# Linear attention with a relu-squared MLP on one core: six chunk pairs instead of four, most of them beside attention, streamed weights, and key sums in turning DVE passes

## The chip, the cores and the metric

The kernel runs on one core of one Trainium2 chip. The metric is the device time of a whole execution in microseconds, the median of several runs. TensorE is called PE, VectorE DVE, ScalarE ACT, GpSimd POOL, and SyncE, which issues most DMAs, SP.

## The reference

```python
def phi(x):                                      # q, k: [8, 8, 576, 64]
    proj = np.einsum('bhsd,df->bhsf', x, w_phi)  # w_phi: [64, 128]
    proj = proj - np.max(np.abs(proj), axis=-1, keepdims=True)
    return np.concatenate([np.exp(proj), np.exp(-proj)], axis=-1)
q_p, k_p = (phi(q), phi(k))
kv = np.einsum('bhsf,bhsd->bhfd', k_p, v)
z = np.sum(k_p, axis=2)
num = np.einsum('bhsf,bhfd->bhsd', q_p, kv)
den = np.einsum('bhsf,bhf->bhs', q_p, z)[..., None] + 1e-06
x = (num / den).transpose(0, 2, 1, 3).reshape(4608, 512)
r = np.maximum(x @ w_in, 0.0)                    # w_in: [512, 2048]
return (r * r) @ w_out                           # w_out: [2048, 512]
```

Attention has no softmax: the key features give a small matrix kv and a vector z, the key sum, for each of the 64 heads. Its output x goes through an MLP of 4608 tokens.

## The kernel before, in words

**Attention** works on 32 pairs of heads. The first six go through `early()`; the other 26 are each spread over *visits* of PE (`visit()`): Q and the key projection of the next pair (L884, L611), the last tokens (L892, L617), then kv of this pair (L669, L674), and the numerators of the pair before (L904). These use half-height or half-width tiles of PE, into the PSUM banks pn, pv, pp and pz. `keys()` takes the key projection out of PSUM, subtracts the largest magnitude and exponentiates (tiles e, and et for the last 64 tokens), and starts the key sums: DVE folds e's token blocks into tile es (L650, L655), and adds et (L660), for each head. `late()` turns es in 32x32 blocks (L966), reduces it to 16 numbers a partition (L967), and sends these through DRAM (zd) and back to be summed into zc (L974). POOL reduces over partitions twice a head: the largest magnitude of a query (L982) and the denominators (L1003). `tokens()` writes x as two float16 halves, high and low, into a *ring* of chunks.

**The MLP** cuts the tokens into 18 chunks of 256 and the hidden columns into 8 steps f of 256. In a plain step (`moe()`) gemm1 makes 24 matmuls with a 128x128 piece of w_in and 256 tokens, float16 in three products of high and low (L1051); ACT takes the relu out of bank ph (L1060); `squares()` makes the square's high part gh on ACT and the low part gl on DVE (a subtraction by the helper at L331); gemm2 adds 12 matmuls of 512 columns to the bank po of the chunk (L1088). A *pair step* (`pair()`) does gemm1 for two chunks at once by seven products of 2x2 blocks instead of eight: 42 matmuls (L1233) instead of 48. It wants sums of blocks of w_in (`add_w()`) and of x (`add_x()`) beforehand, and block sums afterwards: ACT copies one product, DVE makes four adds (L1248), and ACT takes two relus (L1265) before the squares.

Before, 10 chunks are plain and run beside attention; the other 8 form four pairs after it, the first three steps of the first pair being plain. The ring holds 7 chunks, so three of them wait in DRAM (`spill()`, `reload()`). All of w_in stays in two tiles.

**The order of the work** is fixed before the kernel runs: every piece is an operation with the engine, its dependencies, its buffers and a rank, and `Plan` takes for each engine the ready operation of least rank. The ranks come from the table RANKS, two characters an operation. Each engine has its instructions in that one static order, and SP's DMA issues are one such list. Where PE would have stood still early in the program, fillers are put, matmuls on zeros.

## Time and profile before

| what | value |
| --- | --- |
| three runs | 1019.7, 1020.3 and 1021.87 us, median 1020.3 |
| the profiled execution | span 1018.5 us, 1.8 below the median of the runs |
| PE, matmuls | 999.8 us busy, 98% |
| DVE | 763.2 us, 75% |
| ACT | 680.5 us, 67% |
| POOL | 361.2 us, 35% |
| DMA | 77.34 MB, 76 GB/s on the mean |

The span is one execution from its first to its last instruction; busy times come from that execution. An engine's share of busy time is a mean over stages: 0 to 123 us before the first visit, the visits until 705 us, and from there on pairs of chunks alone. Matmuls overlap on PE, so what one costs is read from the distance of two starts.

### The profile page before, as it was taken

How to read it: one execution, taken by the hardware profiler on the slowest of the kernel's cores; microseconds unless marked ns; L12 is line 12 of the kernel's file. 1: busy time of each engine (PE TensorE's matmuls, PEld its weight loads, DVE VectorE, ACT ScalarE, POOL GpSimd, SP SyncE). 2: the span in 40 equal slices, each digit the busy share in tenths (PEclk: the TensorE clock that was granted, in tenths of full speed). 3: DMA queues.
4: the chain of work that ended last, by engine and by line, in shares of the span. 5: the costliest groups of instructions: out<-in, count | busy, mean ns of one | idle time of the engine just before them, and what ended most of it. 6: DMA issues, size and time to landing. Idle time of an engine off the chain costs nothing.

```text
span 1018.5 us, 19261 instructions
## 1 busy us (share of the span) xinstructions
PE 999.8 (98%) x7632; PEld 694.6 (68%) x7713; DVE 763.2 (75%) x1221; ACT 680.5 (67%) x1206; POOL 361.2 (35%) x138
## 2 busy tenths in 40 slices
PE   8999999999999999999999999999999999999998
PEld 4657776776666667666767666666776767677675
DVE  5899878798878989777879888798888447343432
ACT  6989886777777787686777867776555445435444
POOL 2433356364456555475375646563000000000000
PEclk9999999999999999999999999999999999999999
DMA  9754323132322233233324212110002001000001
GB/s 355 282 186 135 122 81 94 39 110 73 85 60 81 75 93 93 60 82 81 107 80 111 83 48 69 41 41 22 13 2 83 1 1 49 14 1 21 22 1 42
DMA packets 94914, 77.34 MB, mean 76 GB/s; under 512 B 58088, under 2 KB 72424, under 8 KB 92776
## 3 DMA queue, kind: packets, MB, share of 16 engines
q1 hardware_dynamic: 94536, 75.59, 24.6%
q8 instruction: 60, 0.98, 0.4%
q10 hardware_dynamic: 288, 0.52, 0.1%
q14 instruction: 30, 0.25, 0.1%
HBM read 61.16 MB, written 14.78 MB: 75 GB/s over the span
## 4 chain that ended last, share of the span: by engine, by line
PE 90%; DVE 3%; DMA 3%; ACT 2%; issue 1%; SPq 0%; DVEq 0%; ACTq 0%
PE po L1088 27%; PE ph L1051 21%; PE pp L1233 7%; PE pz L669 4%; PE pv L1088 4%; PE pn L1088 4%; PE ph L1233 3%; PE pn L904 3%; PE pn L884 2%; PE pp L611 2%; PE pv L904 2%; PE pz L1233 2%; PE pz L674 1%; PE pv L669 1%; PE pz L892 1%
## 5 line engine op out<-in xcount | busy, mean ns | idle before, releaser
L1051 PE MATMUL ph<-ring,win 128*128 128x256 f16 x2064 | 240.4, 273 | 0.8 <-ACT r L1060 0.8
L1051 PEld LDWEIGHTS <-win 128*128 128x128 f16 x2064 | 195.3, 98 | 47.0 <-issue 24.8
L982 POOL PARTITION_ALL_REDUCE mx<-pt x52 | 121.6, 2339 | 122.7 <-ACT pt L335 84.3
L1088 PE MATMUL po<-wh,gh 128*128 128x512 f32 x448 | 143.8, 442 | 0.0
L1003 POOL PARTITION_ALL_REDUCE rb<-rb x26 | 96.5, 3712 | 112.0 <-DVE rb L1000 95.6
L1265 ACT ACTIVATE qe<-qe,cw 128x512 f32<-128x512 f32 x58 | 41.4, 715 | 112.5 <-DVE qe L1248 112.5
L1088 PE MATMUL po<-wl,gl 128*128 128x512 bf16 x448 | 115.1, 379 | 0.0
L331 DVE TENSOR_TENSOR gl<-r,gh 128x512 bf16<-128x512 f32 x86 | 87.5, 1018 | 31.7 <-ACT r L1070 30.7
L1003 POOL PARTITION_ALL_REDUCE ds<-ds x26 | 98.7, 3797 | 25.2 <-DVE ds L1000 24.5
L1088 PE MATMUL po<-wl,gh 128*128 128x512 bf16 x375 | 101.5, 379 | 4.9 <-issue 1.6
L1088 PEld LDWEIGHTS <-gl 128*128 128x128 bf16 x576 | 56.4, 98 | 68.0
L1088 PEld LDWEIGHTS po<-wh,gh 128*128 128x128 f32 x448 | 84.6, 189 | 25.9
L1248 DVE TENSOR_TENSOR qe<-pp,qe 128x512 f32<-128x512 f32 (+1 forms) x87 | 52.3, 602 | 61.3 <-PE pp L1233 59.5
L1060 ACT ACTIVATE r<-ph,cw 128x512 f32<-128x512 f32 x86 | 58.7, 683 | 51.0 <-PE ph L1051 49.3
L331 DVE TENSOR_TENSOR gl<-qe,gh 128x512 bf16<-128x512 f32 x58 | 40.1, 691 | 65.7 <-ACT qe L1070 65.6
L1088 PEld LDWEIGHTS <-gh 128*128 128x128 bf16 x576 | 52.3, 98 | 50.7 <-issue 8.9
L633 ACT ACTIVATE e<-e 128x512 f32<-128x512 f32 x64 | 40.0, 625 | 32.3 <-DVE e L630 32.3
L1233 PEld LDWEIGHTS <-win 128*128 128x128 f16 x522 | 48.8, 98 | 14.2 <-issue 7.8
L1068 ACT ACTIVATE gh<-r 128x512 fp32r<-128x512 f32 x86 | 54.1, 629 | 5.7 <-PE pv L1088 2.0
L1070 ACT ACTIVATE r<-r 128x512 f32<-128x512 f32 x86 | 54.3, 631 | 2.7
L650 DVE TENSOR_TENSOR es<-e 128x512 f32<-128x512 f32 x52 | 46.3, 890 | 4.5 <-ACT e L635 4.3
L669 PE MATMUL pz<-e,v 128*64 128x256 f32 x416 | 49.3, 379 | 0.0
(286 smaller groups left out, 1970.4 us busy)
## 6 DMA issues: line engine op xcount, KB each, us to landing
...
out_dram<-o SPq DMA_DIRECT2D x34, 256.0 KB, 2.1
...
spill<-ring SPq DMA_DIRECT2D x6, 256.0 KB, 2.9
```

Source lines behind the costliest of these rows:

```text
L331: eng.tensor_tensor(out=out_, in0=a, in1=b_, op=ALU.subtract)
L669: PE.matmul(out=to[64 * h:64 * h + 64, 0:256], lhsT=v_[p][:, t, h, :], rhs=e_[2 * p + h][:, t].rearrange("p s f -> p (s f)"), start=t == 0 ...
L904: PE.matmul(out=to[64 * h:64 * h + 64, :], lhsT=kz_[n][:, 128 * s_ + 64 * h:128 * s_ + 64 * h + 64], rhs=qe_[2 * n + h].rearrange("p (s x) ...
L982: o = P.add("POOL", par_us(S), lambda n=n, h=h: G.partition_all_reduce(mx_[n], pt_[p][:, h, :], channels=128, reduce_op=bass_isa.ReduceOp. ...
L1003: o = P.add("POOL", 3.6, lambda y=y: G.partition_all_reduce(y(), y(), channels=128, reduce_op=bass_isa.ReduceOp.add), [o], [home], R(RQ + ...
L1051: PE.matmul(out=ph[:, j, :], lhsT=win[w][:, t, 128 * ff:128 * ff + 128], rhs=at_ring(c, x, t), start=k == 0, stop=k == 3 * KT - 1)
L1060: o = P.add("ACT", act_us(512, 1), lambda: A.activation(out=r_[n], in_=ph_[bank], func=AF.Relu, scale=cw[:, f, 0:1]), [g1], [("ph", bank), ...
L1068: sq = P.add("ACT", act_us(512), lambda: A.activation(out=gh_[n], in_=r(), func=AF.Square), after, use + [("gh", n)], Q)
L1070: o = P.add("ACT", act_us(512), lambda: A.activation(out=r(), in_=r(), func=AF.Square), [sq], use, Q, other=[("DVE", 0.70, lambda: V.tenso ...
L1088: PE.matmul(out=bank(i), lhsT=x[:, j, 128 * i:128 * i + 128], rhs=w[:, j, :], start=turn + j + s == 0, stop=(turn, j, s) == (NFP - 1, 1, 2))
L1233: PE.matmul(out=to, lhsT=fl(x, *al)(k), rhs=fr(y, *ar)(k), start=n == 0, stop=n == 5)
L1248: V.tensor_tensor(out=to, in0=a, in1=b, op=ALU.add)
```

## The change

Key sums: from pair 6 on, three DVE passes take the place of eight instructions. Each is a reduce with `apply_transpose`, which turns 32x32 blocks as it reads them and sums 32 elements: one for each head's e (128x1024 elements), one for et (128x256). The 72 numbers a partition go to zd and come back by two DMAs into the end of kz, and zc is reduced from there. DVE's subtraction for et goes too: ACT exponentiates it from PSUM with a bias, for which it negates the largest magnitude (kmn).

Chunks: 6 are plain, 12 form six pairs, so 48 steps are pair steps and none of these pairs has plain steps. Five pairs (MID) run beside attention, as far as it lasts. Their steps put the seven products into the banks ph, pn, pv and again ph, pn and pv being those of the visits; a copy on ACT takes the first product out, and DVE has one add for each of the other three banks, two for pv. The gh and gl of the pair's second chunk go to DRAM (`put_away()`) and come back (`take_back()`) for its gemm2 after the eight steps of the first. The last pair uses pz, pp and ph, and gemm2 of both chunks directly.

Weights: w_in lies in one tile for each f. It is stored to DRAM (wd), the sums of its blocks are made ahead, half an f at a time, and stored as well (`ahead()`), and `weights()` loads both parts for each pair step, 512 KB each, into two alternating sets of tiles. The ring holds 8 chunks and nothing is spilled. The table RANKS is new and covers all operations; STAY, what a change of tile shape costs a rank, falls from 6 to 0.

Over the whole program there are now 3168 matmuls of gemm1 (1152 plain, 2016 in pair steps) instead of 3282 (2064 and 1218), as many of gemm2 as before, 29 fillers instead of 13, and 713 DMA issues on SP instead of 419. Up to the first visit there are 192 matmuls of gemm1 instead of 168, and the 16 more fillers lie there.

```diff
-RING = 7 * T
+RING = 8 * T
-PAIRED = 10
-PLAIN = 3
-SPILLED = (10, 11, 12)
-PAIRS = ((13, 14), (15, 16), (17, 10), (11, 12))
-TAIL = LEAD + (STEP - 1.0) * PAIRED * NFP
+PAIRED = 6
+PAIRS = [(c, c + 1) for c in range(PAIRED, NCH, 2)]
+MID = 5
...
+        if p >= EARLY:
+            def fold(src, col, k, after, use, rank):
+                sums[p].append(P.add("DVE", dve_us(256 * k), lambda: V.tensor_reduce(
+                    out=col(), in_=src().rearrange("p k (b x) -> p k b x", x=32), op=ALU.add, axis=AX.X, apply_transpose=True),
+                    [after], [use, ("z4", p)], rank))
+
+            for h in range(2):
+                n = 2 * p + h
+                fold(lambda n=n: e_[n].rearrange("p t s f -> p (t s) f"),
+                     lambda h=h: z4_[p][:, :, 0:16].rearrange("p b (u h x) -> p h u x b", u=2, h=2)[:, h],
+                     4, exps[p][h], ("e", n), R(1.0))
+            fold(lambda: et_[p], lambda: z4_[p][:, :, 16:18].rearrange("p b s -> p s b"), 1, exp_t[p], ("et", p), R(1.0))
...
-        o = P.add("DVE", dve_us(512), lambda: V.transpose(es_[p][:, 512:1024], es_[p][:, 0:512]), sums[p], [("es", p)], R(RZ))
-        o = P.add("DVE", dve_us(512), lambda: V.tensor_reduce(
-            out=z4_[p].rearrange("p (b c) -> p c b", c=4), in_=es_[p][:, 512:1024].rearrange("p (c b x) -> p c b x", c=4, x=32), op=ALU.add, axis=AX.X),
-            [o], [("es", p), ("z4", p)], R(RZ))
-
-        o = P.add("SP", 0.4, lambda: SP.dma_start(zd_[p], z4_[p]), [o], [("z4", p), ("zd", p)], R(RZ), land=1.9, xfer=0.1)
-        o = P.add("SP", 0.55, lambda: SP.dma_start(za_[p], zd_[p].rearrange("(a i) (b c) -> (i b) a c", a=4, b=4)),
-                  [o], [("zd", p), ("za", p)], R(RZ), land=2.2, xfer=0.3)
+        w = P.add("SP", 0.4, lambda: SP.dma_start(zd_[p], z4_[p]), sums[p], [("z4", p), ("zd", p)], R(RZ), land=1.9, xfer=0.1)
+        back = []
+        back.append(P.add("SP", 0.5, lambda: SP.dma_start(
+            kz_[p][:, 256:320].rearrange("p (a x) -> p a x", a=4),
+            zd_[p].rearrange("(a i) b x -> (i b) a x", a=4)[:, :, 0:16]), [w], [("zd", p), ("kz", p)], R(RZ), land=2.1, xfer=0.1))
+        back.append(P.add("SP", 0.5, lambda: SP.dma_start(
+            kz_[p][:, 320:328].rearrange("p (a s) -> p a s", a=4),
+            zd_[p].rearrange("(a i) b x -> (i b) a x", a=4)[:, :, 16:18]), [w], [("zd", p), ("kz", p)], R(RZ), land=2.1, xfer=0.2))
         zc = P.add("DVE", 0.23, lambda: V.tensor_reduce(
-            out=zc_[p], in_=za_[p].rearrange("p a c -> p c a"), op=ALU.add, axis=AX.X),
-            [o], [("za", p), ("zc", p)], R(RZ))
+            out=zc_[p], in_=kz_[p][:, 256:328].rearrange("p (y h x s) -> p h s y x", h=2, x=2, s=2), op=ALU.add, axis=AX.XY),
...
+    def weights(f, rank):
+        b = in_pair["step"] = in_pair.get("step", 1) ^ 1
+        o = P.add("SP", 0.45, lambda: SP.dma_start(wo_at(b), wd_[f][0]), [w_stored[f]] + read_o[b], [WO[b]], rank, land=2.4, xfer=1.4)
+        if f in s_stored:
+            s = P.add("SP", 0.45, lambda: SP.dma_start(ws_at(b).rearrange("p k n x c -> p k (n x c)"), wd_[f][1]), s_stored[f] + read_s[b], [WS[b]], rank, land=2.4, xfer=1.4)
+            read_o[b], read_s[b] = [], []
+            return b, [o, s]
...
+    def step(cs, k, turn, f, n, m):
+        g = in_pair["n"] = in_pair.get("n", -1) + 1
+        Q = m - 1000.0
+        rt, r = RT[g % 2], lambda: r_at(g % 2)
+        b, w_ready = weights(f, m - 5.0)
+        product = factors(cs, b)
+        grid = lambda x: x.rearrange("p (j t) -> p j t", j=2)
+        after = w_ready + [parts_x[cs, i] for i in range(2)] + in_pair.get("pe", [])
...
+        i0 = in_pair["ph"]
+        if k < MID:
+            in_pair["ph"] += 2
+            keys = [("ph", i0)], [("pn", ("b", g))], [("pv", ("b", g))], [("ph", i0 + 1)]
+            banks = [lambda: ph_[i0], lambda: grid(pn_["b", g]), lambda: grid(pv_["b", g]), lambda: ph_[i0 + 1]]
+        else:
+            in_pair["ph"] += 1
+            px = ("pp", ("w", g))
+            keys = [("pz", ("w", g))], [px], [px], [("ph", i0)]
+            banks = [lambda: grid(pz_["w", g]), lambda: grid(pp_["w", g][:, 0, :]), lambda: grid(pp_["w", g][:, 1, :]), lambda: ph_[i0]]
+        two = lambda i, x, y: lambda: (product(banks[i]()[:, 0, :], *x), product(banks[i]()[:, 1, :], *y))
+        pa = P.add("PE", 0.66, lambda: product(banks[0]()[:, 0, :], "a11", "b11"), after, keys[0] + reads, m)
+        first, other = copy(T, lambda: r()[:, 1, :], lambda: banks[0]()[:, 0, :])
+        ca = P.add(*first, [pa] + old, keys[0] + [rt], Q - URGENT, other=[other])
+        pb = P.add("PE", 1.31, two(1, ("a12", "b21"), ("s2", "t2")), [pa], keys[1] + reads, m + 0.01)
+        cb_ = P.add("DVE", dve_us(512), lambda: plus(r()[:, 0:4:3, :], banks[1](), wide(r()[:, 1, :])), [ca, pb], keys[1] + [rt], Q - URGENT)
+        pc = P.add("PE", 1.31, two(2, ("s3", "t3"), ("s1", "t1")), [pb], keys[2] + reads, m + 0.02)
+        cc_ = P.add("DVE", dve_us(512), lambda: plus(r()[:, 1:3, :], banks[2](), wide(r()[:, 3, :])), [cb_, pc], keys[2] + [rt], Q - URGENT)
+        c22 = P.add("DVE", dve_us(T), lambda: plus(r()[:, 3, :], banks[2]()[:, 0, :], r()[:, 2, :]), [cc_], keys[2] + [rt], Q - URGENT)
+        pd = P.add("PE", 1.31, two(3, ("a22", "t4"), ("s4", "b22")), [pc], keys[3] + reads, m + 0.03)
+        cd = P.add("DVE", dve_us(512), lambda: plus(r()[:, 1:3, :], banks[3](), r()[:, 1:3, :]), [pd, cc_], keys[3] + [rt], Q - URGENT)
+        in_pair["pe"] = [pd]
...
+            done.append(squares(n + i, lambda i=i: r()[:, 2 * i:2 * i + 2, :], [x], [rt], Q + 0.1 * i))
         in_pair["r", g] = done
+        return done
+
+    gone, read_back = {}, {}
+
+    def put_away(n, k, f, g, rank):
+        def work():
+            SP.dma_start(gd_[k % 2][f][0], gh_[n].bitcast(F32))
+            SP.dma_start(gd_[k % 2][f][1], gl_[n])
+
+        gone[k, f] = P.add("SP", 0.9, work, [g] + read_back.get((k - 2, f), []), [("gh", n), ("gl", n)], rank, land=2.0, xfer=1.1)
+
+    def take_back(n, k, f, rank):
+        def work():
+            SP.dma_start(gh_[n].bitcast(F32), gd_[k % 2][f][0])
+            SP.dma_start(gl_[n], gd_[k % 2][f][1])
+
+        o = P.add("SP", 0.9, work, [gone[k, f]], [("gh", n), ("gl", n)], rank, land=2.2, xfer=1.1)
+        read_back[k, f] = [o]
+        return o
...
+        later = [("po", po0 + 2 + i) for i in range(2)] if mid else [("pn", ("o", k)), ("pv", ("o", k))]
+        po0 += 4 if mid else 2
+        turn_us *= 1.4 if mid else 1.9
+        for j in range(NFP):
+            done = step(cs, k, j, j, n, m)
+            second(n, cs[0], v, j, j, done[0], m + 2.5, po)
+            if mid:
+                put_away(n + 1, k, j, done[1], m)
             else:
...
+                second(n + 1, cs[1], v + 1, j, j, done[1], m + 3.5, later)
+            n += 2
+            m += turn_us
+        used = list(in_pair["pe"])
+        for j in range(NFP if mid else 0):
+            o = take_back(n, k, j, m)
+            second(n, cs[1], v + 1, j, j, o, m + 1.5, later)
+            n += 1
+            m += tick * 0.5
+        v += 2
...
-    "L=6CLUTFEO2uPvAD.-.-Ht3`E*LhX{c?L|81TPLM/%B1.CGQn<cD>of`k:Rv35E9p?e$W-WMWIrtOQ1OhEaM9p48lUaroXtSqqwO"
...
+    "1x3&75;HDe0h0h<07<:>6[@)BS8iE8>>899k<REj>a?B3?4h4n?2@05T<%.T6J6o>{Is?[@2?-6;9S:x>.>Z9O;W=0;*B]BY?*:>"
...
```

**DVE, key sums of a late pair, before.** Names: es folded exponentials, et the last tokens, qe and ds the denominators of other pairs, gl a square of the MLP, z_12 the key sum.

```order
L650 TENSOR_TENSOR es_4663<-e_4601 128x512
L655 TENSOR_TENSOR es_4663<-es_4663 128x256
L660 TENSOR_TENSOR es_4663<-es_4663,et_4625 64x256
L1000 SCALAR_TENSOR_TENSOR rb_4751<-qe_4634,zc_4689,pp_4696 128x576
L966 STREAM_TRANSPOSE es_4663<-es_4663 128x512
L331 TENSOR_TENSOR gl_4762<-r_4748,gh_4753 128x512
L1000 SCALAR_TENSOR_TENSOR ds_4795<-qe_4725,zc_4689,pp_4760 128x576
L967 TENSOR_REDUCE z_12_4815<-es_4663 128x4x4
```

These are the folds of the second head, the transpose and the reduce; the same two folds and the add of the first head stand a few rows earlier.

**DVE, key sums of a late pair, after**, at the same stage of the program; e_4545 and e_4551 are the two heads of one pair.

```order
L628 TENSOR_REDUCE km_4547<-pp_4506 128x4
L631 TENSOR_TENSOR e_4551<-pp_4506,km_4547 128x4x128
L660 TENSOR_REDUCE z_10_4563<-e_4545 128x2x4x4
L650 TENSOR_REDUCE kmt_4576<-pz_4523 128x1
L959 STREAM_TRANSPOSE kvs_4578<-pz_4523 128x256
L660 TENSOR_REDUCE z_10_4563<-e_4551 128x2x4x4
L841 TENSOR_TENSOR rb_4339<-n_4612,rb_4339 128x576
L329 TENSOR_TENSOR qe_4619<-pt_4540,mx_4569 128x576
L660 TENSOR_REDUCE z_10_4563<-et_4582 128x2x4
```

The three rows of L660 with z_10 are all that is left of the sums, and each stands as soon as its e or et is exponentiated.

**DVE, a pair step, before**, after the end of attention (qe_8746 holds the block sums, pp and ph are the banks).

```order
L1248 TENSOR_TENSOR qe_8746<-pp_9815,qe_8746 128x512 x2
L1248 TENSOR_TENSOR qe_8746<-ph_9842,qe_8746 128x512
L1248 TENSOR_TENSOR qe_8746<-pp_9815,qe_8746 128x256
L331 TENSOR_TENSOR gl_9891<-qe_8746,gh_9887 128x512
L1176 TENSOR_TENSOR es_8168<-ring_0_78,ring_1_79 128x2x256
L1176 TENSOR_TENSOR es_8168<-ring_1712 128x2x256
L331 TENSOR_TENSOR gl_9918<-qe_8746,gh_9893 128x512
```

**DVE, a pair step, after**, beside attention: w_1_4650 and w_1_5294 hold the block sums, in the second use of tiles w0 and w1; pn, pv and ph are the banks, and qe_6674, ds_6760 and pt belong to attention.

```order
L329 TENSOR_TENSOR qe_6674<-pt_6375,mx_6599 128x576
L329 TENSOR_TENSOR gl_6699<-w_1_5294,gh_6672 128x512
L1249 TENSOR_TENSOR w_1_4650<-pn_6685,w_1_4650 128x2x256
L1249 TENSOR_TENSOR w_1_4650<-pv_6704,w_1_4650 128x512
L1249 TENSOR_TENSOR w_1_4650<-pv_6704,w_1_4650 128x256
L1249 TENSOR_TENSOR w_1_4650<-ph_6719,w_1_4650 128x512
L329 TENSOR_TENSOR gl_6755<-w_1_5294,gh_6702 128x512
L1006 SCALAR_TENSOR_TENSOR ds_6760<-qe_6674,zc_6657,pp_6737 128x576
L329 TENSOR_TENSOR gl_6789<-w_1_4650,gh_6764 128x512
```

The four adds now stand between a query's subtraction, a denominator's product (L1006) and the squares' subtractions of the step before and of the same step (gl).

**PE, a visit, before**: kv of one pair (pz), the numerators of the pair before (pn, pv), and the next gemm1.

```order
L669 MATMUL pz_5611<-e_5440,v_4402 64x256
L674 MATMUL pz_5611<-et_5446,v_4402 64x256 x2
L904 MATMUL pn_5638<-qe_5448,kz_5481 64x320
L904 MATMUL pn_5638<-qe_5508,kz_5481 64x320
...
L904 MATMUL pv_5639<-qe_5448,kz_5481 64x256
L904 MATMUL pv_5639<-qe_5508,kz_5481 64x256
...
L1051 LDWEIGHTS win_76
L1051 MATMUL ph_5670<-ring_1712,win_76 128x256
```

**PE, a visit, after**: behind kv come the products of a pair step,

```order
L674 MATMUL pz_5809<-e_5487,v_4566 64x256
L674 MATMUL pz_5809<-e_5507,v_4566 64x256
L679 MATMUL pz_5809<-et_5599,v_4566 64x256 x2
L1243 LDWEIGHTS w_1_4901
L1243 MATMUL ph_5839<-ring_1761,w_1_4901 128x256
```

and the numerators follow some hundred rows later, behind a gemm2.

```order
L1075 MATMUL po_5346<-wl_1240,gl_5836 128x512
L1075 MATMUL po_5343<-wh_1232,gh_5828 128x512 x2
L1075 MATMUL po_5346<-wh_1232,gh_5828 128x512 x2
L910 MATMUL pn_5972<-qe_5472,kz_5699 64x320
L910 MATMUL pn_5972<-qe_5530,kz_5699 64x320
...
L910 MATMUL pv_5973<-qe_5472,kz_5699 64x256
L910 MATMUL pv_5973<-qe_5530,kz_5699 64x256
```

In 10 of the 26 visits the numerators are split off so, before in 2.

## Rows read from the trace of the kernel before

**Rows 1.** The page: the span, and each engine's busy time.

```profile
span 1018.5 us, 19261 instructions
PE 999.8 (98%) x7632; PEld 694.6 (68%) x7713; DVE 763.2 (75%) x1221; ACT 680.5 (67%) x1206; POOL 361.2 (35%) x138
```

**Rows 2.** The page: shares of the chain that ended last, by engine.

```profile
PE 90%; DVE 3%; DMA 3%; ACT 2%; issue 1%; SPq 0%; DVEq 0%; ACTq 0%
```

**Rows 3.** Windows: us, then busy us of PE, PEld, DVE, ACT, POOL; clock, DMA share, GB/s.

```profile
0.00:122.60 122.60, 114.78 (x1140) 76.31 (x1148) 101.10 (x173) 105.70 (x184) 40.33 (x32) 0.99 0.63 224
122.60:705.00 582.40, 578.78 (x4498) 402.21 (x4541) 492.19 (x778) 426.59 (x787) 319.50 (x106) 1.00 0.28 75
705.00:782.00 77.00, 74.99 (x495) 53.14 (x500) 66.74 (x108) 39.69 (x61) 1.40 (x1) 1.00 0.10 32
782.00:1018.50 236.50, 231.30 (x1506) 162.97 (x1527) 103.16 (x164) 108.54 (x176) 0.00 (x0) 1.00 0.05 16
350.00:400.00 50.00, 49.52 (x402) 33.73 (x402) 45.93 (x70) 37.06 (x72) 28.36 (x10) 1.00 0.34 89
```

**Rows 4.** PE's timeline in the tail: start, duration, line, operation, count.

```profile
827.40 0.61 PE L1088 MATMUL pn<-wl,gh 128*128 128x512 bf16 x2
...
830.08 0.83 PE L1233 MATMUL pz<-ring,win 128*128 128x256 f16 x6
...
831.40 0.49 PE L1233 MATMUL pp<-k,qe 128*128 128x256 f16 x3
...
832.38 0.49 PE L1233 MATMUL pp<-q,qe 128*128 128x256 f16 x3
```

**Rows 5.** PE's timeline at visit 517: a gemm1, then Q.

```profile
517.79 2.79 PE L1051 MATMUL ph<-ring,win 128*128 128x256 f16 x24
520.51 0.69 PE L884 MATMUL pn<-q,wraw 64*128 64x512 f32 x1
```

**Rows 6.** Groups of DVE in key sums: busy us, mean ns, idle before.

```profile
L650 DVE TENSOR_TENSOR es<-e 128x512 f32<-128x512 f32 x52 | 46.3, 890 | 4.5 <-ACT e L635 4.3
...
L655 DVE TENSOR_TENSOR es<-es 128x256 f32<-128x256 f32 x52 | 39.0, 750 | 1.1
...
L660 DVE TENSOR_TENSOR es<-es,et 64x256 f32<-64x256 f32 x52 | 33.4, 643 | 1.8
...
L967 DVE TENSOR_REDUCE z<-es 128x16 f32<-128x512 f32 x26 | 17.8, 683 | 0.5
...
L953 DVE STREAM_TRANSPOSE kvs<-pz 128x256 f32<-128x256 f32 x26 | 11.6, 444 | 8.9 <-ACT pt L335 6.2 <-PE pz L674 2.2 <-DMA q<-in_qp_dram 0.4
```

**Rows 7.** Groups of DVE in pair steps and sums of chunks.

```profile
L1248 DVE TENSOR_TENSOR qe<-pp,qe 128x512 f32<-128x512 f32 x58 | 40.0, 690 | 60.3 <-PE pp L1233 59.5
...
L331 DVE TENSOR_TENSOR es<-es 128x256 f32<-128x256 f32 x56 | 24.7, 442 | 1.8
...
L1248 DVE TENSOR_TENSOR qe<-pp,qe 128x256 f32<-128x256 f32 x29 | 12.3, 424 | 1.0
...
L1176 DVE TENSOR_TENSOR es<-ring 128x512 f32<-128x512 f16 x12 | 9.3, 802 | 0.1
...
L331 DVE TENSOR_TENSOR v<-es,v 128x1024 f16<-128x1024 f32 x4 | 4.9, 1220 | 1.1 <-ACT v L1136 1.1
```

**Rows 8.** Tiles es and gl on DVE: shortest, median, longest ns.

```profile
L966 DVE STREAM_TRANSPOSE es<-es x26: 693/706/712, 116.3 to 666.6; 128x512 f32<-128x512 f32 x26
...
L331 DVE TENSOR_TENSOR gl<-r,gh x86: 650/692/3050, 89.0 to 722.2; 128x512 bf16<-128x512 f32 x86
...
L331 DVE TENSOR_TENSOR gl<-qe,gh x58: 680/692/694, 731.5 to 1008.8; 128x512 bf16<-128x512 f32 x58
```

**Rows 9.** The squares' subtraction in the groups of DVE.

```profile
L331 DVE TENSOR_TENSOR gl<-r,gh 128x512 bf16<-128x512 f32 x86 | 87.5, 1018 | 31.7 <-ACT r L1070 30.7
```

**Rows 10.** Tile spill: issues; then the DMA list, KB and us to landing.

```profile
L1034 SPq DMA_DIRECT2D ring<-spill x6: 530/626/632, 764.2 to 842.1; - x6
...
ring<-spill SPq DMA_DIRECT2D x6, 256.0 KB, 3.7
```

451 lines of the change are left out of this document (230 added, 221 removed).

## The prediction

> **What bounds the kernel now.** I read the page first: its span is 1018.5 us, and PE is busy for 999.8 us of it, 98%, with DVE at 75% and ACT at 67% [rows 1]. The chain of work that ended last says the same from the other side: followed back from the end it runs through PE for 90% of the span and through DVE and DMA for 3% each [rows 2]. A share of busy time is a mean over stages, so I cut the span at the first visit, at the last numerators and where the pair steps alone remain [rows 3]. PE leaves 7.8 us idle in the first 122.6 us, 3.6 us in the 582 us of attention, 2.0 us in the next 77 us and 5.2 us in the rest; its granted clock is 0.99 to 1.00, so the higher of its two levels, in all of them. In a piece of the attention in which DVE is busy for 45.93 of 50 us PE still idles only 0.5 us [rows 3]. So the time is the number of PE instructions times their spacing, plus some 18 us of gaps, and a change pays only by taking instructions off PE or by keeping the gaps small.
>
> The spacing is read from the starts in PE's timeline, since the durations overlap: nine block products from 831.40 to 832.38, so 0.109 us each, and a whole gemm2 from 827.40 to 830.08, so 2.68 us for 12 matmuls or 0.22 us each [rows 4]. The 24 matmuls of a plain gemm1 take from 517.79 to 520.51 up to the Q of a visit, 2.72 us, where 24 x 0.109 = 2.62 would do: a switch into the half-height tiles of attention costs about 0.1 us [rows 5].
>
> **The change, part by part.** *Products.* A plain chunk spends 24 matmuls per step f, a pair 42 where two plain chunks spend 48. Before there are 86 plain steps (2064 matmuls) and 29 pair steps (1218), after 48 plain (1152) and 48 pair steps (2016): 3282 become 3168, 114 fewer. The second product, 1728 matmuls, does not change. 114 x 0.109 = 12.4 us, and PE has nothing to overlap them with, so all of it is on the path: **-12.4**.
>
> *The head.* Up to the first visit the new order has 24 more products and 16 more fillers. If the products only fill idle time (7.8 us there), up to 24 x 0.109 = 2.6 us are won; if the fillers stand where work could have stood, up to 16 x 0.22 = 3.5 us are lost. A filler is put where PE would have waited, so I take **-1.0**.
>
> *Splits.* The numerators follow their visit's kv at once in 24 of 26 visits now and are split off in 2; after the change 16 and 10. Eight more splits, each two more switches of 0.1 us [rows 5]: **+1.6**, between 0 and 3.
>
> *Key sums on DVE.* Now the folds, the transpose and the reduce take 46.3 + 39.0 + 33.4 + 17.8 us over 26 pairs, and the transpose, 0.706 us each, another 18.4: 154.9 us, 5.96 us a pair [rows 6, 8]. No row of before shows a reduce that turns blocks as it reads. Nearest are the plain transposes: 0.706 us for 512 elements, 0.444 us for 256, so 1.02 ns an element, and 0.706 + 512 x 0.00102 = 1.23 us for 1024. Two of these and one of 0.44 make 2.90 us a pair, 75.5 us in all. The bounds: a transpose and a reduce one after the other, 1.23 + 1.2, would make 5.7 us a pair; nothing reads less than once, so 2.9 is also about the floor. I take the floor, since it is one pass in the instruction. **DVE -79 us.**
>
> *The rest of DVE.* 19 more pair steps at three adds of 0.690 and one of 0.424 us, 2.49 us: +47. Two more pairs need four more halves of chunk sums, each 2 x 0.802 + 4 x 0.442 + 1.22 = 4.6: +18 [rows 7]. The sums of w_in handle the same elements in 64 more instructions; what an instruction costs beyond its elements is 2 x 0.444 - 0.706 = 0.18 us: +12. DVE's total stays within 3 us of 763, but it has a longer attention stretch to lie in: after the last numerators PE has only 16 pair steps and 40 gemm2, 16 x 42 x 0.109 + 40 x 2.68 = 180 us, so attention ends near 830 us and no longer at 705. DVE's share there falls from 0.845 to about 0.82, ACT's stays at about 0.73, and the sum takes nothing from either: PE hides both.
>
> *Pair steps beside attention.* This is the new thing: 14 visits, before none, now come while pair steps run, and a step's four banks are emptied by a chain of ACT, DVE, DVE, DVE, DVE. PE's share of gaps is 0.6% in the attention stretch and 2.6% in the 77 us in which the pair steps begin now, with the chunk and weight sums before them [rows 3]. The stretch concerned is 14/26 of (830 - 123), 380 us; the difference of 2.0% makes 7.6 us at most, and 0 at least, if the cover holds. The first three steps of the stretch are like those 77 us, the rest is steadier: **+3.8**, half of it.
>
> *Streams.* w_in and its sums come back from DRAM, 1 MB a step, and the second chunk's gh and gl of 40 steps go out and return: DMA moves some 87 MB more. 0.63 of the engines' time for 224 GB/s [rows 3] makes 356 GB/s, so 245 us of all 16 engines, spread over 700 us: the share beside attention rises from 0.28 to about 0.6. A step's weights take 1.05/356 = 2.9 us and a landing, and a step with its two gemm2 takes PE 42 x 0.109 + 2 x 2.68 = 9.9 us, double buffered. Cover for the weights is ample; I count **0**.
>
> Sum: -12.4 - 1.0 + 1.6 + 3.8 = -8.0; 1018.5 becomes 1010.5 in the profiled execution. The median of the runs, 1020.3, lies 1.8 us above that span, so the forecast is **1012 us**.
>
> **The rule beside the row.** Of two DVE instructions that run beside POOL's reductions, the square's subtraction with two operands in SBUF has a median of 0.692 us and a longest of 3.05, and its twin that runs after POOL is done never passes 0.694; the transpose, with one operand, runs beside the same reductions and never passes 0.712 [rows 8]. So an instruction with two operands in SBUF is held, one with a single one is not, and the passes that go are of the first kind and those that come of the second. The Trainium skill (SBUF — State Buffer, "Who interferes with whom") has this as a rule: DVE and GpSimd share one pair of ports, and the second SBUF input of a DVE instruction comes through it; these rows agree. By the rule the new passes would be free of holds altogether, and the sum would be the same, since DVE's time is hidden. For the turning pass itself the skill (Vector Engine (DVE) Microarchitecture Reference, 3.8) says that the 32x32 transpose in front of the datapath sustains one element per cycle and lane; an estimate from this is 1.07 us for 1024 elements, near the 1.23 that I use; no run here shows it yet.
>
> **Rivals.** *A, slower: evacuations held up by POOL.* A bank of a pair step is wanted again one step's part later. Its DVE add (one operand in PSUM, so not held itself) stands in DVE's queue behind the subtraction of a square, which is. The mean hold of that subtraction is 1.018 - 0.692 = 0.33 us (87.5 us over 86 in the groups) [rows 8, 9], and a step has two. The cover is one gemm2 less an add, 2.68 - 0.69, 2.0 us, and the longest hold is 2.36 us. For it: the cover is shorter than the longest hold, and banks pn and pv are shared with the visits. Against it: POOL is busy for 55% of the stretch, and PE lost 0.5 us in 50 with DVE at 92%. Without waits the run would be 1012 - 3.8 = 1008.3; if both holds are felt in the 32 steps beside attention, 32 x 0.66 = 21 us make 1029. It passes 1020.3 from 0.37 us a step.
>
> *B, slower: gh and gl come back late.* A square's buffers (three) are freed by a gemm2 and wanted two gemm2 later, 5.4 us. A return, 256 KB of gh and 128 KB of gl, is nearest to a spilled chunk's: 0.63 us for an issue, and 3.7 us from issue to landing [rows 10]. The second DMA follows the first by an issue, 4.3 us in all, so it holds with 1.1 us to spare. On a busier queue, behind weights, it is late from a landing of 4.8 us on; 0.3 us more make 40 x 0.3 = 12 us and 1020.3, and 0.5 us make 1028.
>
> *C, faster: no waits and a fuller head.* With gaps at 0.6% throughout and -2.6 in the head: 1018.5 - 12.4 - 2.6 + 0 + 1.8 = 1005.3.
>
> *D, no change in kind: the turning passes read at half rate.* At 5.7 us a pair DVE has 73 us more and a share near 0.92; the 50 us above show that PE bears it, so it only adds to A's chance.
>
> **How the numbers follow.** The forecast, 1008 to 1016, has a chance of 0.66; C 0.06; A 0.13; B 0.10; something that I have not seen, of either sign, 0.05. The range leaves out half of C's tail and the upper parts of A and B: **1003 to 1025**. A measurement of this kernel tells about 0.2%, 2 us, from no change: faster is below 1018.3, slower above 1022.3. The forecast and C are faster, 0.72 and a little of the rest; A from 0.37 to 0.43 us a step and B near 0.3 us are within; so faster 0.73, same 0.09, slower 0.18.
>
> **What would show it.** Right: PE's busy time near 988 to 992 us, 3168 products at 0.109; key-sum passes of 1.2 and 0.44 us with a longest near the median; PE's idle time before the block products small and named after DVE; attention's end near 830. Wrong in the largest term only if PE's gaps exceed 18 + 12 us: idle time of PE before the block products that ends with DVE's add (A), or before gemm2 that ends with a DMA (B), or a granted clock under 0.99 after some idle stretch.

## The result, and the profile after

The changed kernel is slower: 1034.58 us (four runs, 1031.54 to 1035.52), against 1020.53 us for the kernel before, a ratio of 1.0134 (95% interval 1.0116 to 1.0153). The prediction was 1012 us, between 1003 and 1025, so its sign was wrong, and the time lies above its range. The profiled execution has a span of 1032.5 us where the sum gave 1010.5; 22 us are to be explained.

The page of the kernel after, its span, busy times and chain that ended last:

```profile
span 1032.5 us, 19744 instructions
PE 997.7 (97%) x7529; PEld 685.8 (66%) x7615; DVE 749.1 (73%) x1233; ACT 684.6 (66%) x1252; POOL 356.2 (34%) x141
PE 77%; DVE 5%; DMA 5%; ACT 4%; issue 1%; SPq 1%; POOL 0%; DVEq 0%; ACTq 0%
```

Beside [rows 1, 2], DVE has 14 us less, where its terms in the prediction make 2 us less, and PE 2 us less, where 988 to 992 us was named as the sign of being right; and the chain, which ran through PE for 90% of the span, now does so for 77%. The windows, in the columns of [rows 3], cut at the first Q (137.3 us; 123.2 before), the last numerators, 77 us later, and the end:

```profile
0.00:137.30 137.30, 122.44 (x1199) 80.63 (x1207) 104.95 (x172) 105.86 (x185) 48.79 (x37) 1.00 0.56 198
137.30:844.80 707.50, 694.65 (x5196) 481.55 (x5256) 563.00 (x931) 500.62 (x937) 304.31 (x105) 1.00 0.53 158
844.80:921.80 77.00, 75.75 (x508) 54.19 (x513) 41.96 (x69) 34.78 (x61) 3.09 (x1) 1.00 0.56 184
921.80:1032.50 110.70, 104.87 (x633) 69.47 (x639) 39.23 (x63) 43.32 (x71) 0.00 (x0) 0.99 0.34 117
```

The clock is at its higher level throughout. PE leaves 14.9 us idle in the head (7.8 before) and 12.9 us in attention (3.6 before); what follows attention idles for 7.1 us, as the two stretches before did (7.2). Of PE's matmuls 86 are missing from this trace and 81 from that of before (PE's count against PEld's), and a missing one counts as idle time. The same order of PE with every record is in the trace of e2_sums, an experiment below; there the attention of the kernel before idles for 1.1 us:

```profile
122.60:300.00 177.40, 176.93 (x1391) 121.43 (x1389) 120.22 (x194) 130.68 (x244) 93.01 (x33) 1.00 0.31 79
300.00:500.00 200.00, 199.41 (x1580) 137.99 (x1579) 138.02 (x229) 147.94 (x279) 107.26 (x37) 1.00 0.33 85
500.00:705.00 205.00, 205.00 (x1566) 142.17 (x1564) 152.74 (x231) 147.57 (x266) 110.53 (x38) 1.00 0.26 67
```

From the first Q to the end the kernel takes 895.2 us, before 895.3. There the prediction's terms make -9.6: 138 products fewer (114, and 24 that went into the head) at 0.109 are -15.0, splits +1.6, waits +3.8. So **9.5 us** are missing behind the first Q. Up to it the terms make +1.6 (24 products, 2.6, less 1.0), and 14.1 were measured: **12.5 us** are missing in the head. Half of what the head's window is longer than that of [rows 3], 14.7 us, is more busy time of PE (7.7), half more idle time (7.0).

What went as predicted: the new passes and pair steps in the groups of DVE, and the subtraction of the squares by tile (shortest/median/longest ns), which answer [rows 6 to 9]:

```profile
L660 DVE TRANSPOSE_TENSOR_REDUCE z<-e 128x32 f32<-128x1024 f32 x52 | 64.0, 1238 | 1.1 <-ACT e L636 0.8
...
L1249 DVE TENSOR_TENSOR w<-pn,w 128x512 f32<-128x512 f32 x40 | 27.5, 687 | 25.6 <-PE pn L1243 22.9 <-ACT w L1057 2.3 <-ACT gh L1055 0.3
...
L660 DVE TRANSPOSE_TENSOR_REDUCE z<-et 128x8 f32<-128x256 f32 x26 | 11.2, 431 | 0.2
```

```profile
L329 DVE TENSOR_TENSOR gl<-w,gh x96: 642/684/2790, 442.7 to 1023.8; 128x512 bf16<-128x512 f32 x96
L329 DVE TENSOR_TENSOR gl<-r,gh x48: 641/691/3116, 96.6 to 434.5; 128x512 bf16<-128x512 f32 x48
```

The key sums are 75.2 us where 75.5 were forecast. The products keep their distance: in PE's timeline beside attention groups of six start 0.67 and 0.65 us apart, 0.11 a product, as in [rows 4].

```profile
477.51 0.83 PE L1243 MATMUL ph<-ring,w 128*128 128x256 f16 x6
478.18 0.82 PE L1243 MATMUL pn<-ring,w 128*128 128x256 f16 x6
478.83 0.82 PE L1243 MATMUL pn<-w,w 128*128 128x256 f16 x6
```

New are waits with a round trip through DRAM in them. PE's and DVE's lists of waits (us in total, times, longest), and the landings that answer [rows 10] (KB, us):

```profile
PE pn L1243 <- DVE pt L334: 2.3, 1, 2.3
PE po L1075 <- DMA gh<-gd: 2.2, 4, 1.0
```

```profile
DVE rb L841 <- DMA rb<-rd: 31.3, 13, 5.8
```

```profile
w<-wd SPq DMA_DIRECT2D x96, 512.0 KB, 4.4
...
gh<-gd SPq DMA_DIRECT2D x40, 256.0 KB, 3.3
```

L841 is the product of the numerators with the inverse denominators, which come back by rb<-rd; before it waited for 8.2 us in 5. The longest stall of PE shows how such a wait travels. DVE's timeline, then PE's:

```profile
484.30 0.76 DVE L841 TENSOR_TENSOR rb<-n,rb 128x576 f32<-128x576 f32 x1 [2.15 <-DMA rb<-rd]
...
489.37 0.65 DVE L334 COPY pt<-pn 128x512 f32<-128x512 f32 x1
```

```profile
490.07 0.71 PE L1243 MATMUL pn<-ring,w 128*128 128x256 f16 x5 [2.27 <-DVE pt L334]
```

DVE stands for 2.15 us at 484; behind it, after eight other instructions, comes the copy that empties the visit's bank pn, and the pair step that wants pn is 2.27 us late.

### The profile page after: what moved, and what is told of

Same layout as the page of the kernel before. It is cut to its first block, busy times and chain, and to the rows that moved or that the text cites. A ratio compares the mean times of both kernels' runs of the same rounds, so it can differ in the third digit from the quotient of the medians.

```text
span 1032.5 us, 19744 instructions
## 1 busy us (share of the span) xinstructions
PE 997.7 (97%) x7529; PEld 685.8 (66%) x7615; DVE 749.1 (73%) x1233; ACT 684.6 (66%) x1252; POOL 356.2 (34%) x141
## 4 chain that ended last, share of the span: by engine, by line
PE 77%; DVE 5%; DMA 5%; ACT 4%; issue 1%; SPq 1%; POOL 0%; DVEq 0%; ACTq 0%
PE po L1075 29%; PE ph L1038 11%; PE ph L1243 8%; PE pn L1243 5%; PE pv L1243 5%; PE pz L674 4%; PE pn L890 2%; PE pn L910 2%; PE pp L1243 2%; PE pp L612 2%; PE pv L910 2%; DMA gh<-gd 1%; DMA kz<-zd 1%; PE pn L1075 1%; PE pv L1075 1%
## 5 line engine op out<-in xcount | busy, mean ns | idle before, releaser
L1243 PEld LDWEIGHTS <-w 128*128 128x128 f16 x2016 | 193.5, 98 | 43.2 <-issue 19.0
L1038 PE MATMUL ph<-ring,w 128*128 128x256 f16 x1152 | 134.5, 273 | 0.5 <-ACT r L1047 0.5
L1038 PEld LDWEIGHTS <-w 128*128 128x128 f16 x1152 | 109.1, 98 | 25.7 <-issue 13.1
L1294 ACT ACTIVATE w<-w,cw 128x512 f32<-128x512 f32 x96 | 67.8, 714 | 87.1 <-DVE w L1249 87.1
L329 DVE TENSOR_TENSOR gl<-w,gh 128x512 bf16<-128x512 f32 x96 | 77.3, 809 | 60.6 <-ACT w L1057 60.4
L1055 ACT ACTIVATE gh<-w 128x512 fp32r<-128x512 f32 x96 | 60.3, 628 | 26.9 <-issue 9.1
L1243 PE MATMUL ph<-ring,w 128*128 128x256 f16 x528 | 72.4, 273 | 0.8 <-DVE w L1249 0.8
L660 DVE TRANSPOSE_TENSOR_REDUCE z<-e 128x32 f32<-128x1024 f32 x52 | 64.0, 1238 | 1.1 <-ACT e L636 0.8
L1057 ACT ACTIVATE w<-w 128x512 f32<-128x512 f32 x96 | 60.5, 630 | 2.9
L329 DVE TENSOR_TENSOR gl<-r,gh 128x512 bf16<-128x512 f32 x48 | 40.3, 842 | 28.5 <-ACT r L1057 28.0
L1243 PE MATMUL pv<-w,w 128*128 128x256 f16 x480 | 60.2, 276 | 0.0
L329 DVE TENSOR_TENSOR qe<-pt,mx 128x576 f32<-128x576 f32 x52 | 54.0, 1038 | 6.6 <-POOL mx L988 3.3
```

The lines of the kernel that those rows point to most:

```text
L329: eng.tensor_tensor(out=out_, in0=a, in1=b_, op=ALU.subtract)
L660: sums[p].append(P.add("DVE", dve_us(256 * k), lambda: V.tensor_reduce(out=col(), in_=src().rearrange("p k (b x) -> p k b x", x=32), op=AL ...
L1038: PE.matmul(out=ph[:, j, :], lhsT=w_[f][0][:, w, t, 128 * j:128 * j + 128], rhs=at_ring(c, x, t), start=k == 0, stop=k == 3 * KT - 1)
L1055: sq = P.add("ACT", act_us(512), lambda: A.activation(out=gh_[n], in_=r(), func=AF.Square), after, use + [("gh", n)], Q)
L1057: o = P.add("ACT", act_us(512), lambda: A.activation(out=r(), in_=r(), func=AF.Square), [sq], use, Q, other=[("DVE", 0.70, lambda: V.tenso ...
L1243: PE.matmul(out=to, lhsT=fl(x, *al)(k), rhs=fr(y, *ar)(k), start=n == 0, stop=n == 5)
```

## Experiments

All ratios are to the kernel before on the same chip; the kernel after has 1.0134. Differences in us are those of the ratios, times 1020.5. A profiled span is one execution and scatters by some 3 us, so ratios decide.

**e1_head.** The order of everything up to the first visit is taken from the kernel before, as a list HEAD of operation, engine and place; the rest keeps the order of the kernel after. 192 products stay in the head; the fillers, which are put where the order has gaps, become 13 instead of 29 (by their weight loads; 24 of the 29 matmuls are recorded in the trace of after).

```diff
     order = P.improve()
...
+    for op in order:
+        if op.n in head:
+            op.take(head[op.n][0])
+            op.start, op.end, op.there = head[op.n][1]
```

> The changed kernel, with everything up to the first visit put in the order (and on the engines) that it has in the kernel before; the rest keeps the changed order. Theory 'head order': the new order table makes the six early pairs and the preparation of the weights wait for one another, so the first visit starts at 137.3 us where 123.2 plus one more plain product (2.6) would do. Then the first visit comes at 126 to 128 us and the run takes 1022 to 1026 us. Rival: the head is late from what the change adds to it (tiles of w_in by f, four v buffers in place of five, shared buffers); then the first visit stays later than 133 us and the run above 1030.

1024.91 us, 1.0047 (1.0028 to 1.0065): 8.9 us are won back, and the first Q is at 129.7. From there to the end it is 895.2 us, unchanged. The head's order, with the fillers that came with it, was a cause of its own, and the waits behind it another.

**e2_sums.** The kernel before with the key sums alone.

```diff
-            o = P.add("DVE", dve_us(512), lambda n=n: V.tensor_tensor(
+            o = P.add("DVE", dve_us(512), lambda n=n, h=h: turned(
```

> The kernel before, with the key sums alone changed: for each late pair the folds, the transpose and the plain reduce are gone and three turning passes (and two small loads in place of one) come in; all else keeps its order. Forecast of the prediction: DVE's busy time falls by about 79 us and the time stays, 1018 to 1021 us, since PE hides it. Rival: DVE's queue does hold PE up somewhere, then it gets faster than 1017; or the two small loads are late, then it gets slower than 1023.

1023.08 us, 1.0030 (1.0020 to 1.0040), 3 us slower and not the same, though DVE falls from 763.2 to 681.9 us. PE's last matmul is only 0.6 us later than before, so up to there PE hid what DVE saved; the rest of the 3 us lies behind it, in the issue of the last output transfer on ACT's queue (2.44 us for 0.38). I don't know whether this belongs to the change.

**e3_thin.** The kernel after with thin streams: 64 KB of weights instead of 512 KB from the third step on, a sixteenth of the squares put away from the third pair on.

```diff
-        o = P.add("SP", 0.45, lambda: SP.dma_start(wo_at(b), wd_[f][0]), ...
+        o = P.add("SP", 0.45, lambda: SP.dma_start(cut(wo_at(b)), cut(wd_[f][0])), ...
```

> The changed kernel with thinner streams: from the third pair step on each load of weights carries 64 KB in place of 512 KB, and from the third pair on a put-away carries a sixteenth of gh and gl; so weights and squares are those of earlier steps and the output is not the reference's. Every transfer is still issued, at the same place and after the same waits. Theory 'bandwidth' (the streams slow down each other and attention's small transfers): the time falls by 5 us or more, to 1024 to 1029. Theory 'queue' (SP issues in order and waits for a square or a bank ahead of attention's small transfers): it stays within 2 us of the changed kernel, 1032 to 1036.

1029.6 us, 1.0094 (1.0075 to 1.0112): 4.1 us. The stall of 2.27 us shrinks to 0.4, DVE's waits for rb only to 28.2 us. Bytes are a part.

**e4_late.** The kernel after with the issues that put squares away moved back by up to 3 us in SP's queue.

```diff
+    for op in gone.values():
+        op.start = max(op.start, min([op.start + 3.0] + ends))
```

> The changed kernel with the put-away issues moved back in SP's order by up to 3 us of planned time (never past the next use of their buffer), so that attention's small transfers are issued ahead of them; the same work and bytes. Theory 'queue': DVE's waits for rb<-rd (31.3 us in all) fall by half, the 2.4 us stall of PE before pn at 487 us goes, and the time falls by 3 to 6 us, to 1028 to 1032. Theory 'bandwidth': within 2 us of the changed kernel.

1.0163 (1.0137 to 1.0189), no gain, and DVE's waits for rb fall only to 27.7 us: this place in SP's queue was not the cause.

**e5_pool and e6_both.** e1_head with POOL's reductions for the denominators over 96 of 576 columns, which tests rival A; then the same with thin streams.

```diff
-                y(), y(), channels=128, reduce_op=bass_isa.ReduceOp.add), ...
+                y()[:, 0:96], y()[:, 0:96], channels=128, reduce_op=bass_isa.ReduceOp.add), ...
...
-            V.tensor_scalar(out=den_[p], in0=den_[p], scalar1=1e-6, scalar2=None, op0=ALU.add)
+            V.tensor_scalar(out=den_[p], in0=den_[p], scalar1=1e30, scalar2=None, op0=ALU.max)
```

> The kernel of e1_head with the denominators' reductions of POOL over 96 of their 576 columns (the rest is not reduced, and a floor of 1e30 under the denominator keeps the quotient finite, so the output is not the reference's). POOL is then busy for about half as long. Theory POOL (rival A of the prediction: DVE's subtractions, held while POOL reduces, make the evacuations and the copies beside them late): the stalls of PE from the first visit on, some 14 us beyond the spacing of its instructions, lose at least a third, and the span goes from 1024.9 to 1018 to 1021. Theory DMA (the waits are for round trips through DRAM: DVE for the ring's rows, PE for the squares that come back): POOL takes no part, so the span stays within 2 us of 1024.9, and DVE's waits for the ring's rows stay near 30 us.

> e5_pool with thin streams: weights of 64 KB instead of 512 KB from the third pair step on, and a sixteenth of the squares put away from the third pair on. Theory DMA, by bytes: another 5 us go, as the thin streams took 5 from the kernel after (1034.6 to 1029.6), so 5 below e5_pool. Theory POOL: the two causes are apart and add, so this is e1_head less 5 for the streams less what e5_pool gave, 1013 to 1016. Theory order (the waits come from the one fixed order, in which a queue stands behind a late instruction whatever made it late): less than 3 us below e5_pool, and some 8 us of stalls remain.

e5_pool: 1017.24 us, 0.9974 (0.9962 to 0.9986), 7.5 below e1_head; e6_both: 1013.72 us, 0.9946 (0.9931 to 0.9961), 2.9 less. The attention windows of e1_head, e5_pool and e6_both:

```profile
129.70:836.40 706.70, 696.99 (x5257) 480.58 (x5256) 565.67 (x932) 502.02 (x938) 306.36 (x106) 1.00 0.53 158
```

```profile
127.50:826.40 698.90, 696.02 (x5257) 480.78 (x5256) 516.77 (x933) 501.92 (x938) 169.07 (x106) 1.00 0.53 160
```

```profile
126.40:823.90 697.50, 695.17 (x5257) 480.67 (x5256) 517.46 (x933) 501.79 (x938) 168.33 (x106) 1.00 0.39 109
```

All three traces have every record. PE's work is the same, 695 to 697 us; its idle time is 9.7, 2.9 and 2.3. POOL's reductions are the larger lever, but they do two things: they hold DVE's instructions, and they end late. The next runs take these apart.

**e7_split, e8_aftersplit, e9_beforesplit, e10_split2.** Each reduction for the denominators is issued as three of 192 columns, in e1_head, after and before; in e10_split2 that for the largest magnitude is in two pieces as well.

```diff
-            o = P.add("POOL", 3.6, lambda y=y: G.partition_all_reduce(
-                y(), y(), channels=128, reduce_op=bass_isa.ReduceOp.add), ...
+            o = P.add("POOL", 3.6, lambda y=y: [G.partition_all_reduce(
+                y()[:, i:i + 192], y()[:, i:i + 192], channels=128, reduce_op=bass_isa.ReduceOp.add) for i in range(0, S, 192)][-1], ...
```

> e1_head with each of POOL's 52 reductions for the denominators issued as three of 192 columns instead of one of 576; nothing is left out. In the profile of e1_head a DVE subtraction with two operands in SBUF that starts in the first 2.4 us of such a reduction ends 0.45 to 0.52 us before POOL's does, however early it began, and one with less than 1.0 us of it left is not held. Theory holds: a subtraction then waits for the rest of one short reduction, 1.5 us by the line through 0.98 us for 96 columns and 3.7 for 576, so for about 0.5 to 1.0 us instead of up to 2.4; the span goes from 1024.9 to 1016 to 1018, although POOL is busy for longer, 52 x 0.9 = 45 us more. Theory latency (what was won in e5_pool is the earlier end of the denominators, which the numerators wait for): the reductions end later, so 1025 or more.

> The kernel after with the same split of POOL's reductions, its own head. Theory holds, with a head that is a cause of its own: the gain is that of e7_split over e1_head, so 1034.6 less 7 to 9, some 1026.5, and about 2 us of that in the head. Were head and holds one cause, it would gain more here, 10 us or above.

> The kernel before with the same split. Its subtractions are held as well (1.018 us on the mean for 0.692), but its PE idles for only 3.6 us in 582 us of attention: theory holds with cover says that the holds are hidden there, so 1018.5 to 1020, no measurable gain or one of up to 2 us. If the holds were simply added to the path, with or without pair steps, it would gain as e7_split does, 7 us.

> e7_split with the 52 reductions for the largest magnitude in two halves of 288 columns as well. In e1_head these hold a subtraction in their first 1.1 of 2.1 us, until 0.30 us before they end. Theory holds: 1 to 2 us below e7_split. Against: what a piece costs beyond its columns, 0.4 us each, makes the numerators' tokens later, which would take it back: within 1 us of e7_split.

1.0034 (1.0017 to 1.0052), 1.0148 (1.0120 to 1.0176), 0.9991 (0.9978 to 1.0005) and 1.0050 (1.0032 to 1.0068): nothing anywhere. The holds did shrink (the mean of gl<-w from 818 to 749 ns, of the subtraction for qe from 987 to 812). So either they did not matter, or the 0.8 us by which the split lengthens a reduction took the gain back.

**e11_poolq and e12_splitq.** e1_head and e7_split with the transfers of the denominators on POOL's own queue.

```diff
-            dens.append(P.add("SP", 0.4, lambda y=y, h=h: SP.dma_start(
+            dens.append(P.add("SP", 0.4, lambda y=y, h=h: G.dma_start(
```

> e1_head with the 52 small transfers of the denominators' results issued on POOL's own DMA queue, behind the reduction that they wait for, instead of on SP's, where all later issues stand behind them; the order of everything else is the same. SP waits for these reductions for 41.9 us between 430 and 840 us in e1_head, 61.6 in e7_split and next to nothing in e5_pool. Theory SP queue (what e5_pool won is that loads and returns on SP no longer stand behind a wait for POOL): SP's wait for POOL goes, PE's waits for gh from gd (3.0 us in 4) go too, and the span falls from 1024.9 to 1018 to 1021. Theory latency (the numbers of the denominators come later than their users): within 2 us of 1024.9, as the transfers still come after the reductions.

> The same issue on POOL's queue, with the reductions in three pieces as in e7_split. If holds of DVE and the queue of SP are the two parts of what e5_pool won (10.8 us of span), and the split won the one and lost the other by 20 us more of SP's waits, this is 1014 to 1018. If the later end of the longer reductions is what e7_split lost by, it stays near 1023.

1.0042 (1.0029 to 1.0055) and 1.0049 (1.0031 to 1.0068). SP no longer waits for POOL, and the time stays: this theory fell too. The wait turned up on DVE, for the denominators themselves: 13.1 us in 9 in e11_poolq and 36.0 in 15 in e12_splitq, for 2.1 in 1 in e1_head.

**e13_busy, e14_one, e15_zero.** e13_busy is e5_pool with a second reduction behind each, whose result nobody reads; e14_one is e1_head with gl made by a pass of one operand; e15_zero has only the data of e5_pool.

```diff
+                y()[:, i:j], y()[:, i:j], channels=128, reduce_op=bass_isa.ReduceOp.add) for i, j in ((0, 96), (96, 480))][-1]
...
-        return P.add("DVE", 0.70, lambda: sub(V, gl_[n], r(), gh_[n].bitcast(F32)),
+        return P.add("DVE", 0.70, lambda: plain(gl_[n], r()),
```

> e5_pool with POOL kept busy: behind each denominators' reduction of 96 columns follows a second one over 384 columns whose result nobody reads, so that POOL is busy as long as in e1_head (3.6 us for 3.7) and DVE's subtractions are held as there, while the denominators leave POOL after 1.0 us (their transfers and the steps behind take the first of the 96 columns only; the output is not the reference's). Theory latency (e5_pool won because the denominators came 2.7 us earlier): the span stays near 1014, 1013 to 1017. Theory POOL's time (holds of DVE, and the next reduction, for the largest magnitudes, standing behind this one in POOL's queue): it goes back to 1021 to 1025.

> e1_head with the 144 subtractions that make gl replaced by a pass of one operand in SBUF (a sum over one element each: gl becomes the square rounded, the high part is not taken off, so the output is not the reference's). POOL's work and every order stay. Theory holds (a subtraction with two operands in SBUF is held, and what stands behind it on DVE is late): the held time of these goes without any change in POOL's times, and the span falls by the larger part of 10.8 us, to 1015 to 1018; e7_split then failed because it made each reduction 0.8 us longer. Theory latency or POOL's queue: 1022 to 1025, as DVE's holds do not matter.

> e1_head with the floor of 1e30 under the denominators alone, as in e5_pool and e13_busy, and with POOL's reductions whole: x is then next to zero (the output is not the reference's). Control of the data. If the gain of e5_pool and e13_busy came from their zeros, this is at 1015 to 1018; if from POOL's earlier results, it stays at 1024 to 1026.

e13_busy: 0.9975 (0.9956 to 0.9995); e14_one: 1.0056 (1.0038 to 1.0073); e15_zero: 1.0037 (1.0023 to 1.0050). POOL is as busy in e13_busy as in e1_head (184.6 us for 192.8 in these reductions) and the gain is still whole. In e14_one no pass for gl is held any more, and nothing is won (shortest/median/longest ns):

```profile
L330 DVE TENSOR_REDUCE gl<-w x96: 645/678/689, 435.6 to 1014.9; 128x512 bf16<-128x512 f32 x96
L330 DVE TENSOR_REDUCE gl<-r x48: 634/685/687, 90.8 to 427.0; 128x512 bf16<-128x512 f32 x48
```

But e13_busy didn't keep the holds of e1_head, as it was meant to. DVE's three groups of subtractions that are held, in e1_head, e7_split and e13_busy (busy us, mean ns):

```profile
L329 DVE TENSOR_TENSOR gl<-w,gh 128x512 bf16<-128x512 f32 x96 | 78.3, 818 | 61.7 <-ACT w L1057 59.7 <-PE ph L1243 1.9
L329 DVE TENSOR_TENSOR qe<-pt,mx 128x576 f32<-128x576 f32 x52 | 51.3, 987 | 7.2 <-POOL mx L988 3.5 <-PE pv L910 2.4 <-PE ph L1038 0.5
L329 DVE TENSOR_TENSOR gl<-r,gh 128x512 bf16<-128x512 f32 x48 | 43.3, 903 | 27.5 <-ACT r L1057 27.1
```

```profile
L329 DVE TENSOR_TENSOR gl<-w,gh 128x512 bf16<-128x512 f32 x96 | 71.7, 749 | 65.7 <-ACT w L1057 64.9 <-DMA w<-wd 0.7
L329 DVE TENSOR_TENSOR qe<-pt,mx 128x576 f32<-128x576 f32 x52 | 42.2, 812 | 10.2 <-POOL mx L988 7.3 <-PE pv L910 2.0 <-PE ph L1038 0.5
L329 DVE TENSOR_TENSOR gl<-r,gh 128x512 bf16<-128x512 f32 x48 | 38.2, 797 | 33.4 <-ACT r L1057 33.2
```

```profile
L329 DVE TENSOR_TENSOR gl<-w,gh 128x512 bf16<-128x512 f32 x96 | 70.9, 741 | 64.4 <-ACT w L1057 62.0 <-PE ph L1243 1.9 <-DMA w<-wd 0.4
L329 DVE TENSOR_TENSOR qe<-pt,mx 128x576 f32<-128x576 f32 x52 | 41.5, 797 | 6.9 <-POOL mx L988 3.6 <-PE pv L910 2.6
L329 DVE TENSOR_TENSOR gl<-r,gh 128x512 bf16<-128x512 f32 x48 | 39.2, 818 | 37.1 <-ACT r L1057 37.0
```

They sum to 172.9 us in e1_head, 152.1 in e7_split and 151.6 in e13_busy; in e14_one the passes in their place make 151.1, with qe still held (1029 ns on the mean). So three runs are rid of some 21 us alike, and only e13_busy wins. What tells it from the other two is the moment at which the denominators leave POOL: after 0.89 us, against 3.6 in e14_one and three times 1.51 in e7_split. So it is that moment; not the holds alone, not POOL's time, not the data. No single run excludes that the holds of qe count together with POOL's time: they are gone in e13_busy, gone in e7_split beside a POOL that is busy for 50 us more than in e13_busy, and there in e14_one.

**e16_late3 and e17_late6.** e1_head with all that follows the reductions (transfers, inverse, L841, the ring's rows) 3 or 6 us later in its queues, where the users leave room.

```diff
+            op.start = max(op.start, min([op.start + 3.0] + [x.start - 0.02 for x in nexts.get(op.n, ())]))
```

> e1_head with the whole computation and another order: everything that follows POOL's reductions of a pair (transfer of the denominators, their inverse, its way through DRAM, the product with the numerators and the ring's rows) stands 3 us later in the queues of SP, DVE and ACT, wherever its users leave room. Theory latency (the results of POOL come later than the order has it, and the queues of SP and DVE stand still behind steps that wait for them): the steps wait less although nothing ends earlier, and the time falls from 1024.9 to 1016 to 1020. Theory without the order (the denominators are wanted early by someone): 1025 or more.

> The same by 6 us. Theory latency: DVE's waits for the ring's rows, 26 us in 11 at present with a longest of 5.4, go nearly all; the time is that of e16_late3 or up to 3 us below it. If 3 us were enough, or the later ring makes a chunk late, it is the same or above.

1.0183 (1.0161 to 1.0205) and 1.0409 (1.0389 to 1.0428): 14 and 37 us slower. In e16_late3 DVE's waits for rb between 137 and 840 us fall from 20.5 to 12.5, and it is slower all the same: less of the largest new wait in the trace did not make it faster. These runs also put DVE's steps among others, so they do not show that the lateness alone costs this.

**e18_beforepool.** The control: e5_pool's edit in the kernel before.

> The kernel before with POOL's reductions for the denominators over 96 of 576 columns, as in e5_pool (the output is not the reference's). Control in the other kernel: does it pay as well to have the denominators 2.7 us earlier where no pair steps stand beside attention? Theory latency with cover: the plain steps cover it; PE idles for 3.6 us in 582 us of attention, so this gains 0 to 3 us, 1017 to 1020. If the latency of the denominators bounds both kernels alike, it gains the 7.5 us of e5_pool, 1013, and is no explanation of what the change lost.

1019.31 us, 0.9993 (0.9983 to 1.0002): 0.7 us, not told from none. Where plain steps stand beside attention, the same 2.7 us a reduction are hidden.

## Why the prediction was wrong

**Products: right, within 1 us.** With both causes of waiting nearly gone, e6_both takes 885.2 us from the first Q to the end; the sum makes 895.3 - 9.6 = 885.7. That sum has 3.8 us of waits in it, so PE's busy time says more: behind the first Q it is 876.8 us in e6_both and 889.5 in e2_sums, both with every record, 12.7 less where products and splits together make 13.4. e6_both leaves work out, but none of PE's. The sign of 988 to 992 us of busy time failed all the same, with 997.7: the head took 7 us more.

**Key sums: right.** 1238 ns for 1.23 us, 431 for 0.44, the longest 1374 and 573. PE hides it, as e2_sums shows up to its last matmul. DVE's total, 749.1 us where 763 was expected, is off by 14 us: the subtraction for et, 7.4 us before, had no term, and L841 takes 24.2 us for 32.1. For the turning pass the Trainium skill (Vector Engine (DVE) Microarchitecture Reference, 3.8) gives one element per cycle and lane; the 1238 ns for 1024 elements here agree with an estimate of 1.07 us from it and 0.17 us besides.

**The head: wrong by 12.5 us.** "A filler is put where PE would have waited, so I take -1.0" put both into idle time and took the order around them as free. But PE is busy for some 7 us longer up to the first Q, about what 24 products and 16 fillers cost by the prediction's own figures (2.6 and 3.5), and its idle time grew by 7 us instead of shrinking. With the order of the kernel before, the same products and 13 fillers 8.9 us come back. How much of it is the fillers (an estimate of 3.5 us, 16 x 0.22) and how much the order was not taken apart: no run has one without the other. PE's longest waits up to the first Q are spread over DVE, ACT and the loads, 1 to 2 us each. Kernels with that head still reach the first Q 3 to 6.5 us later than 123.2; 2.6 of them would be the 24 products.

**Pair steps beside attention: mis-sized.** "+3.8, half of it", with 7.6 as the most, came from the idle share of 77 us in which no visit stands beside pair steps. That was no bound: the wait that counts there did not exist in that stretch. Where every record is there, PE's idle time in attention rose from 1.1 us (e2_sums) to 9.7 (e1_head), 8.6 us where the term had 3.8, and 6.8 of it go when the denominators leave POOL 2.7 us earlier; the kernel's time falls by 7.5 us, in this kernel and not in the one before (e5_pool, e13_busy, e18_beforepool). By which steps their lateness reaches PE, stall for stall, I could not settle: of the two visible waits behind it, taking away SP's (e11_poolq) or part of DVE's (e16_late3) won nothing. And DVE's waits for rb, the largest new ones, stay where the gain is whole: 26.0 us in e1_head, 24.2 in e5_pool, 27.6 in e13_busy. Moving the loads of the weights to another queue was not tried.

**Streams: wrong.** "I count 0": their bytes cost 4.1 us in the kernel after and 2.9 without POOL's lateness. The cover was counted for the weights themselves; what their traffic does to the small round trips beside them was left out. One of these, zd<-z, lands after 1.7 us for 2.7 in e3_thin and 1.8 for 2.6 in e6_both; that the bytes cost their time by this way is not shown.

**Rival A** named POOL rightly, and the wrong property of it. Its price was for held subtractions. They are held, as foretold, by up to 2.4 us; but e14_one, e7_split and e13_busy are alike rid of some 21 us of it, and only the last, whose denominators leave POOL early, wins. The Trainium skill (SBUF — State Buffer, "Who interferes with whom") has the second SBUF operand of a DVE instruction come through ports shared with GpSimd; the runs agree with that, down to the pass of one operand whose longest is 689 ns where the subtraction's is 3116. It does not follow that a hold costs time. **Rival B** is seen only in small: PE waits for gh from DRAM 2.2 us in 4, not 0.3 us a step. **D** is excluded by the 1238 ns.

Together the head's order with its fillers (8.9), the denominators' lateness (7.5) and the bytes (2.9) are 19.3 of the 22 us. No version that does the whole work beats the kernel before; the nearest are e9_beforesplit, which is its equal, e2_sums at 1.0030, and of those with more pair steps e7_split at 1.0034.
